# Two batches' agents in one key-score matmul, the agents' load put first, and a new order of the queues

## Chip, core and metric

The kernel runs on one core of a Trainium2 chip, as one launch. The metric is device time in microseconds of one execution; the kernel before takes 1118.79 us (median of 3 runs, 1118.47 to 1120.4).

## What is computed

Two stages, all in float32, for 2 batches of 12480 tokens with 128 channels and 49 agents per batch:

```python
scale = 1.0 / np.sqrt(128)
def sm(a, b):                               # softmax over b's rows
    s = scale * (a @ b.transpose(0, 2, 1)); s = s - s.max(-1, keepdims=True)
    e = np.exp(s); return e / (e.sum(-1, keepdims=True) + 1e-09)
agent_v = sm(agents, k) @ v                 # 49 x 128 per batch
x = (sm(q, agents) @ agent_v).reshape(24960, 128)
h = x @ w_in                                # 2048 wide
g = np.where(h >= 1, h, np.where(h <= -1, 0.0, (h + 1) ** 2 / 4))
out = g @ w_out
```

The kernel never forms x: it multiplies agent_v into w_in once per batch, and x @ w_in becomes (softmax of a query tile) times that product.

## The kernel before

**Stages.** For batch 0 the key phase (`keys_phase`) goes over the 98 subtiles of 128 keys in 14 groups of 7. A group's keys are loaded into one of four `kbuf` buffers (L453); `scores` (L473) multiplies each subtile, as the stationary operand, with the 49 agent columns `ag[:, b, :]` as the moving operand, into columns t*49 to t*49+49 of a PSUM tile. ScalarE copies the 343 columns out (`evac`, L284), VectorE takes their maximum (L485, L493). After the seventh group, and again after the last, the maximum over all keys is formed by a transpose (L515), a reduction, a diagonal matrix and a matmul (L528), so that GpSimd can subtract it (L567) and ScalarE take the exponential (L574). Then `av` (L582) multiplies the weights of each subtile (98 stationary columns) with 129 columns of `vbuf` (values and a column of ones; four buffers, L562), and VectorE adds the group's sum to `acc` (L598). `weights` normalizes (L621 to L623), transposes (L626), forms agent_v times w_in in four matmuls of 512 columns (L646) and splits the result into a high and a low part (L284, L658).

**Tiles.** Then 49 tiles of 512 tokens follow. `queries` loads a tile of q (L681), computes its scores against the agents (L686) and the softmax (L699 to L730), transposes it (L739). `pair` runs eight times per tile: `g1` (L782) makes 256 columns of h in a `ph` tile (three buffers of two PSUM banks); ScalarE does L789 and L794, VectorE L797; `g` is split into `ghi` (L284 on ScalarE, L288 on VectorE or L286 on GpSimd) and `glo` (L808, VectorE or GpSimd), and `g2h`, `g2l` (L818) accumulate three products in one of two PSUM banks. Batch 1's key phase runs in pieces between the pairs of batch 0's tiles, on the PSUM banks, with the same lines (`bank` in the profile in place of `ph`). Some preparation stands beside batch 0's key phase: `load_raw` (L405) fetches w_in and w_out as 64-bit words, and `decode` (L347 to L382) turns them into float32 on VectorE and GpSimd.

**Order.** Every step is an `Op` in `Order`; `run` puts the steps in one sequence by the time at which they could start in a planner's account, and among those by a key. `PRO`, `START` and `NEXT` hold the keys of the beginning and of batch 1, `KEYS0` and `KEYS1` those of the tiles of either batch, `HI_ENG` and `LO_ENG` the engine for each pair's split ("*" leaves it to the planner). Each engine then executes its instructions in that order. All loads and stores go through one queue, on SyncE (SP), which issues in order too and waits for a buffer where one is still in use. `warm` (L427) multiplies seven bf16 tiles of zeros at the very start.

A float32 matmul of the program stands as two records in the profile, each with a weight load of its own (98 matmuls of L473 per batch, 196 records).

Of the kernel before, what the change touches and what calls it, by code (L numbers as in the profile page):

```python
# [19 lines left out]
SUB = 128  # L20
# [3 lines left out]

HI_ENG = (("PA*P**DD", "DADAPPDA",), ("*DD*DDD*", "DPADDADD",))
LO_ENG = (("DDD*DD*P", "DDPDDDPD",), ("*PDD*PDD", "*DDD*D*D",))


ENG = dict(norm="PD", ql="P", qh="AD", mc="A", out="AD", sub="PD", evac="A")


KEYS0 = dict(g1=1.0, relu=9.2, square=-6.8, gate=11.9, hi=0.3, lo=-7.5, g2=8.3, g2l=6.0,
             out=19.0, q=-4.5, qm=-4.1, qe=28.0, qt=13.8, qn=34.9, qh=13.2, ql=-31.0, tr=13.9,
             mc=1.3)
KEYS1 = dict(g1=-1.4, relu=8.0, square=6.2, gate=8.7, hi=1.4, lo=-38.6, g2=11.0, g2l=-5.7,
             out=73.6, q=-4.4, qm=-27.9, qe=5.0, qt=2.6, qn=-4.0, qh=10.4, ql=3.9, tr=8.9,
             mc=28.3)
KEY = (KEYS0, KEYS1)  # L40


START = dict(raw0=-23.7, raw1=-33.2, raw2=-0.5, raw3=-25.1, out0=33.3, out1=100.6, out2=122.6,
             out3=110.6, q0=-50.6, q1=1.3, q2=145.1, v=9.6, dec=119.9, dout=240.7, km=32.2,
             qs0=85.1, qs1=101.4, qs2=186.4, sub=101.3, av=179.2, w=16.1, pm=108.3, split=7)


NEXT = dict(k=-30.3, v=171.3, s=0.7, step=2.8, m=81.8, av=92.2, avstep=6.7, sub=110.8, w=3.9)
WARM = 7
BUFS = dict(k=4, v=4, q=4, qs=3, m=2, g=5, hi=5, lo=5, o=2, wf=2, h=3)  # L50

# [35 lines left out]
class Order:  # L87
# [5 lines left out]
    def add(self, choices, fn, deps=(), key=0.0, acq=(), rel=()):  # L93

        if isinstance(choices[0], str):
            choices = (choices,)
        choices = tuple((e, us, bool(port)) for e, us, *port in choices)
        op = Op(len(self.ops), choices, fn, deps, key, acq, rel)
        self.ops.append(op)
        return op  # L100
# [82 lines left out]
def agent_attention_moe(  # L183
# [15 lines left out]
    nc = tc.nc  # L199
    C, NTOK = qT.shape  # L200
    B = kT.shape[0]
    A = agT.shape[2]
# [7 lines left out]
    A2 = 2 * A  # L210
# [21 lines left out]
    half = const.tile([128, 1], F32, name="half")  # L232
    idle = const.tile([128, 512], BF16, name="idle")
    ag = const.tile([128, B, A], F32, name="ag")
    win = const.tile([128, FF], F32, name="win")
    wo_hi = const.tile([128, NC, 128], F32R, name="wo_hi")
    wo_lo = const.tile([128, NC, 128], F32R, name="wo_lo")
# [27 lines left out]
    NSX = T // 128  # L265
    native = sorted({p for b in HI_ENG for e in b for p in range(NP) if e[p] == "N"})
    wo = {p: const.tile([128, 2, 128], F32, name=f"wo{p}") for p in native}
# [11 lines left out]
    add = od.add  # L279
# [20 lines left out]
    def one(ps):  # L300
        return ps if len(ps.shape) == 2 else ps[:, 0, :]
# [118 lines left out]
    PRO = -2000.0  # L420
# [9 lines left out]

    warm_op = add(("PE", 0.43 * WARM), warm, [first], PRO - 1, ("h",))
    warm_op.rel = (("h", warm_op),)
    ld_ag = add(("DMA", 0.2), lambda o, e: nc.sync.dma_start(out=ag, in_=agT), (), PRO - 0.5)


    def keys_phase(b, k_key, v_key, s_key, m_key, a_key, e_key, p_key=0.0, wait=None):

        on_bank = b > 0
        last, av_ops = None, []
        LK, LV, KX, KE = {}, {}, {}, {}  # L440
        first_of = [0] if b else [0, START["split"]]
        pms, mxs = [], []
# [4 lines left out]
        def part(g):  # L447
            return sum(g >= x for x in first_of) - 1
        for g in range(NG):
            kb = kbuf[(b * NG + g) % BUFS["k"]]  # L450

            def fn(o, e, g=g, kb=kb, h=slice(0, KG * SUB)):
                nc.sync.dma_start(out=kb[:, h], in_=kT[b, :, g * KG * SUB:][:, h])  # L453

            rest = []
            if b or g:
                LK[g] = load(128 * KG * SUB * 4, fn, (), k_key(g), ("k",))
            else:
                n, m = HALF * SUB, KG * SUB
                LK[g] = load(  # L460
                    128 * n * 4, lambda o, e, fn=fn: fn(o, e, h=slice(0, n)), (), k_key(g) - 1.0,
                    ("k",),
                )
                rest = [load(
                    128 * (m - n) * 4, lambda o, e, fn=fn: fn(o, e, h=slice(n, m)), (), k_key(g)
                )]

            def scores(o, e, g=g, kb=kb, lo=0, hi=HALF):
                if lo == 0:
                    area(o, ("k", b, g))  # L470
                ps = one(PS["k", b, g])
                for t in range(lo, hi):
                    nc.tensor.matmul(  # L473
                        out=ps[:, t * A:(t + 1) * A], lhsT=kb[:, t * SUB:(t + 1) * SUB],
                        rhs=ag[:, b, :], start=True, stop=True,
                    )

            def scores2(o, e, scores=scores):
                scores(o, e, lo=HALF, hi=KG)

            def evac(o, e, g=g):
                copy(e, ksf[:, g, 0:KG * A], one(PS.pop(("k", b, g)))[:, 0:KG * A])

            def gm(o, e, g=g):
                dve.tensor_reduce(  # L485
                    out=gmax[:, g % 2, :] if g else pms[0],
                    in_=ks[:, g, 0:KG, :].rearrange("p t a -> p a t"),
                    axis=AX.X,
                    op=ALU.max,
                )  # L490

            def gm2(o, e, g=g):
                dve.tensor_tensor(  # L493
                    out=pms[part(g)], in0=pms[part(g - 1)], in1=gmax[:, g % 2, :], op=ALU.max
                )

            x = add(("PE", 0.21 * HALF), scores, [LK[g], ld_ag], s_key(g))
            back = take(x, on_bank)
            y = add(("PE", 0.21 * (KG - HALF)), scores2, [x, *rest], s_key(g), (), (("k", LK[g]),))
            KE[g] = add(  # L500
                elementwise("evac", KG * A), evac, [y, *([wait[g]] if wait else [])], s_key(g) + 1, (), (back,)
            )
            KX[g] = add(("DVE", 0.42), gm, [KE[g]], s_key(g) + 1.1)
            if g:
                KX[g] = add(("DVE", 0.13, 1), gm2, [KX[g], KX[g - 1]], s_key(g) + 1.1)

        mb_ops, rescale = [], None
        for i in range(len(first_of)):

            pm, mx, mb = pms[i], mxs[i], mbs[i]  # L510
# [46 lines left out]
        for g in range(NG):  # L557
            vb = vbuf[(b * NG + g) % BUFS["v"]]
            s = ks[:, g, 0:KG, :]
# [40 lines left out]
            k = a_key(g)  # L600
# [70 lines left out]
    def queries(j):  # L671
        st, kk = {}, KEY[turn(j)]
        key = (j - 2) * NP + kk["q"] if j > 2 else PRO + START[f"qs{j}"]
        n, bl = width(j), blocks(j)
# [72 lines left out]

        lq = load(128 * n * 4, ld, (), key - 24 if j > 2 else PRO + START[f"q{j}"], ("q",))
        qs = add(("PE", 0.224 * ns), scores, [lq, ld_ag], key, ("qs",), (("q", lq),))
# [17 lines left out]
    def pair(j, p, w_ops, wo_op):  # L767
        s = j * NP + p
        st, kk = {}, KEY[turn(j)]
        hi_e, lo_e = plan(HI_ENG, j)[p], plan(LO_ENG, j)[p]  # L770
        n = width(j)
# [40 lines left out]
        def product(terms):  # L812
            for w, f, x, c in terms:
                first_mm = LEFT.get(j) is None
                if first_mm:
                    LEFT[j] = sum(2 if e == "N" else 6 for e in plan(HI_ENG, j))
                LEFT[j] -= 1
# [46 lines left out]
    def output(j):  # L864
# [19 lines left out]
        lambda g: PRO + g,  # L884
        lambda g: PRO + START["v"] + g,
        lambda g: PRO + 20 + g,
        PRO + START["km"],
        lambda g: PRO + START["av"] + 2 * g,
        lambda g: PRO + START["sub"] + 2 * g,
# [15 lines left out]
    for n in range(2):  # L905
        for h in range(2):
# [25 lines left out]
            k = PRO + START["dout"] + 2 * n + h  # L932
# [76 lines left out]
```

## Time and profile before

| | |
|---|---|
| median of 3 runs | 1118.79 us |
| the profiled execution | 1119.35 us, span 1117.6 us |
| PE busy | 1098.8 us, 98% of the span |
| ACT, DVE busy | 997.6 us, 993.6 us (89% each) |
| POOL busy | 589.1 us (53%) |
| moved by DMA | 56.57 MB, mean 51 GB/s |
| batch 0's key scores on PE | 10.15 to 57.17 us |
| batch 0's L582 on PE | 57.17 to 85.3 us |
| first L782 | 93.90 us |

The span runs from the first to the last instruction; the execution's own time is 1.75 us longer. PE's busy time counts modelled ends of pipelined matmuls, so the pace of a stretch is better read from the chain of waits, which gives the start, the length and the number of records of each piece.

### The profile page before, as it was taken

To read this page: it belongs to the slowest core of one execution; us is meant where nothing else is said; L and a number is where in the kernel's file an instruction comes from. 1 tells how busy PE (TensorE), PEld (TensorE's weight loads), DVE (VectorE), ACT (ScalarE), POOL (GpSimd) and SP (SyncE) were. 2 spreads that over 40 slices of the span, in tenths; PEclk is the share of its full clock that TensorE was granted. 3 is DMA by queue.
4 is the path that set the end of the run, shared out by engine and by line. 5 is a ranking of instruction groups with operands and counts; after the bars stand their busy time and mean duration, and the time that the engine had idled before them with its cause. 6 is when DMAs were issued, how large, how long until landed. Compare 5 with 4: busy or idle time off the path is not lost.

```text
span 1117.6 us, 15009 instructions
## 1 busy us (share of the span) xinstructions
PE 1098.8 (98%) x5357; PEld 911.0 (82%) x5357; DVE 993.6 (89%) x1203; ACT 997.6 (89%) x1165; POOL 589.1 (53%) x363
## 2 busy tenths in 40 slices
PE   7998999999999999999999999999999999999998
PEld 6986888888878887888878888888888888888776
DVE  5448898899998999988899989999999999999998
ACT  1226998999999999999989999999999999999997
POOL 2153554446577575455456464555555465565544
PEclk9998999999999999999999999999999999999999
DMA  7674221001001111211000000110010011000000
GB/s 237 232 259 146 69 69 38 28 19 38 20 29 52 55 50 39 63 36 45 29 20 29 29 29 19 30 38 20 19 39 20 23 34 36 10 10 20 10 20 17
DMA packets 23691, 56.57 MB, mean 51 GB/s; under 512 B 2752, under 2 KB 3136, under 8 KB 23616
## 3 DMA queue, kind: packets, MB, share of 16 engines
q1 hardware_dynamic: 23616, 55.60, 15.2%
q8 instruction: 43, 0.70, 0.3%
q14 instruction: 32, 0.26, 0.1%
HBM read 42.81 MB, written 12.78 MB: 50 GB/s over the span
## 4 chain that ended last, share of the span: by engine, by line
PE 90%; ACT 4%; DVE 3%; DMA 1%; issue 1%; SPq 0%; DVEq 0%; ACTq 0%
PE bank L818 45%; PE ph L782 31%; PE ph L473 4%; PE bank L686 3%; PE bank L473 2%; PE ph L582 2%; ACT g L789 2%; PE bank L582 2%; ACT g L794 1%; PE bank L739 1%; DVE g L797 1%; DVE glo L808 1%; ACT ghi L284 1%; DMA ag<-agT 1%; PE ph L646 1%
## 5 line engine op out<-in xcount | busy, mean ns | idle before, releaser
L808 POOL TENSOR_TENSOR glo<-g,ghi 128x1024 fp32r<-128x1024 f32 (+1 forms) x147 | 387.4, 2635 | 324.0 <-DVE ghi L288 281.3
L797 DVE SCALAR_TENSOR_TENSOR g<-g,ph 128x1024 f32<-128x1024 f32 (+1 forms) x392 | 467.0, 1207 | 55.6 <-ACT g L794 48.8
L789 ACT ACTIVATE g<-ph,half 128x1024 f32<-128x1024 f32 (+1 forms) x392 | 428.7, 1113 | 27.8 <-PE ph L782 25.5
L794 ACT ACTIVATE g<-g 128x1024 f32<-128x1024 f32 (+1 forms) x392 | 407.3, 1061 | 2.4
L782 PE MATMUL ph<-mt,w_hi 98*128 98x512 f32 (+3 forms) x800 | 317.9, 399 | 2.5 <-DVE g L797 2.3
L808 DVE TENSOR_TENSOR glo<-g,ghi 128x1024 fp32r<-128x1024 f32 (+1 forms) x245 | 312.3, 1300 | 3.0 <-ACT ghi L284 2.2
L782 PE MATMUL ph<-mt,w_lo 98*128 98x512 f32 (+3 forms) x800 | 312.4, 391 | 0.0
L818 PE MATMUL bank<-ghi,wo_hi 128*128 128x512 f32 (+1 forms) x784 | 249.5, 399 | 2.4 <-DVE acc L598 1.8
L818 PE MATMUL bank<-glo,wo_hi 128*128 128x512 f32 (+1 forms) x784 | 243.2, 395 | 0.9 <-POOL glo L808 0.9
L818 PE MATMUL bank<-ghi,wo_lo 128*128 128x512 f32 (+1 forms) x784 | 243.7, 392 | 0.0
L782 PEld LDWEIGHTS ph<-mt,w_hi 98*128 98x128 f32 x800 | 150.9, 189 | 40.1 <-DVE g L797 6.2
L782 PEld LDWEIGHTS ph<-mt,w_lo 98*128 98x128 f32 x800 | 151.6, 189 | 31.6 <-issue 0.2
L818 PEld LDWEIGHTS bank<-ghi,wo_lo 128*128 128x128 f32 x784 | 147.3, 188 | 33.1
L818 PEld LDWEIGHTS bank<-glo,wo_hi 128*128 128x128 f32 x784 | 145.2, 188 | 33.3 <-POOL glo L808 1.4
L818 PEld LDWEIGHTS bank<-ghi,wo_hi 128*128 128x128 f32 x784 | 142.6, 189 | 32.2 <-DVE acc L598 2.2
L288 DVE CAST ghi<-g 128x1024 fp32r<-128x1024 f32 (+1 forms) x199 | 139.5, 719 | 1.0
L284 ACT ACTIVATE ghi<-g 128x1024 fp32r<-128x1024 f32 (+1 forms) x122 | 128.6, 1055 | 4.6 <-DVE g L797 4.5
L286 POOL CAST ghi<-g 128x1024 fp32r<-128x1024 f32 x71 | 89.4, 1260 | 71.4 <-DVE g L797 47.0
L730 POOL TENSOR_TENSOR pq<-qd,pq 128x196 fp32r<-128x196 f32 (+1 forms) x49 | 37.3, 761 | 44.6 <-ACT pq L284 33.7
L686 PEld LDWEIGHTS bank<-ag,qt 128*128 128x128 f32 x368 | 47.9, 191 | 4.2 <-DVE acc L598 0.2
L473 PE MATMUL ph<-ag,kbuf 128*128 128x49 f32 x196 | 43.0, 413 | 5.8 <-DMA ag<-agT 5.8
L473 PEld LDWEIGHTS ph<-ag,kbuf 128*128 128x128 f32 x196 | 42.4, 332 | 6.8 <-DMA kbuf<-kT 6.7
(86 smaller groups left out, 609.4 us busy)
## 6 DMA issues: line engine op xcount, KB each, us to landing
vbuf<-v_in SPq DMA_DIRECT2D x28, 451.5 KB, 4.2
qt<-qT SPq DMA_DIRECT2D x48, 256.0 KB, 2.6
outT<-ot SPq DMA_DIRECT2D x48, 256.0 KB, 2.0
kbuf<-kT SPq DMA_DIRECT2D x27, 448.0 KB, 3.4
raw<-w_in SPq DMA_DIRECT2D x4, 512.0 KB, 6.6
raw<-w_out SPq DMA_DIRECT2D x4, 512.0 KB, 6.1
kbuf<-kT SPq DMA_DIRECT2D x1, 256.0 KB, 7.2
kbuf<-kT SPq DMA_DIRECT2D x1, 192.0 KB, 7.5
```

Source lines behind the costliest of these rows:

```text
L284: act.activation(out=out, in_=in_, func=ACTF.Copy)
L286: pool.tensor_copy(out, in_)
L288: dve.tensor_copy(out, in_)
L473: nc.tensor.matmul(out=ps[:, t * A:(t + 1) * A], lhsT=kb[:, t * SUB:(t + 1) * SUB], rhs=ag[:, b, :], start=True, stop=True,)
L582: nc.tensor.matmul(out=one(PS["v", b, g])[0:A2, 0:C + 1], lhsT=ksf[:, g, t * A:t * A + A2], rhs=vb[:, t, :], start=t == 0, stop=t == KG - 1,)
L686: nc.tensor.matmul(out=ps[lo:hi, i * A:(i + 1) * A], lhsT=st["q"][:, i * 128 + lo:i * 128 + hi], rhs=ag[:, b, :], start=True, stop=True,)
L782: nc.tensor.matmul(out=st["h"][:, c, lo:hi], lhsT=w[:, f:f + 128], rhs=M[j][:, lo:hi], start=(i == 0), stop=(i == 1),)
L789: act.activation(out=st["g"], in_=st["h"][:, :, 0:n], func=ACTF.Relu, bias=half, scale=0.5)
L794: act.activation(out=st["g"], in_=st["g"], func=ACTF.Square)
L797: dve.scalar_tensor_tensor(out=st["g"], in0=st["g"], scalar=1.0, in1=st["h"][:, :, 0:n], op0=ALU.min, op1=ALU.max,)
L808: (pool if e == "POOL" else dve).tensor_tensor(out=st["lo"], in0=st["g"], in1=st["hi"].bitcast(F32), op=ALU.subtract)
L818: nc.tensor.matmul(out=bank[j % 2][:, 0:n], lhsT=w[:, f, :], rhs=x[:, c, :], start=first_mm, stop=LEFT[j] == 0,)
```

## The change

`scores` moves 98 columns through each stationary key subtile in batch 0, both batches' agents side by side, and 49 as before in batch 1. Column block t*49 to t*49+98 is written; its second half is written again by the next subtile's matmul, and after the seventh it is not read. The load of the agents gets the first place of all (key 2*PRO in place of PRO - 0.5). The tables of the order and of the engines are filled with other numbers.

```diff
@@ tables
-HI_ENG = (("PA*P**DD", "DADAPPDA",), ("*DD*DDD*", "DPADDADD",))
+HI_ENG = (("P*P*PPD*", "PAD**DDA",), ("PDDPPDDA", "PP*DP*DA",))
...
@@ agent_attention_moe
     ag = const.tile([128, B, A], F32, name="ag")
+    agf = ag.rearrange("c b a -> c (b a)")
...
-    ld_ag = add(("DMA", 0.2), lambda o, e: nc.sync.dma_start(out=ag, in_=agT), (), PRO - 0.5)
+    ld_ag = add(("DMA", 0.2), lambda o, e: nc.sync.dma_start(out=ag, in_=agT), (), 2 * PRO)
...
                 ps = one(PS["k", b, g])
+
+
+                n = A if on_bank else A2
                 for t in range(lo, hi):
                     nc.tensor.matmul(
-                        out=ps[:, t * A:(t + 1) * A], lhsT=kb[:, t * SUB:(t + 1) * SUB],
-                        rhs=ag[:, b, :], start=True, stop=True,
+                        out=ps[:, t * A:t * A + n], lhsT=kb[:, t * SUB:(t + 1) * SUB],
+                        rhs=agf[:, b * A:b * A + n], start=True, stop=True,
                     )
```

Five lines come in ahead of most of the code, so that L473 of before is L478 now, L582 is L587, L686 is L691, L782 is L787 and L818 is L823. By engine the splits of `g` now stand thus: `ghi` 107 on ScalarE, 131 on VectorE, 154 on GpSimd (before 122, 199, 71), `glo` 282 on VectorE and 110 on GpSimd (before 245 and 147).

**PE, from the first matmul on real data into the key scores** (`kbuf_106` to `kbuf_109` are the four key buffers). Before:

```order
L473 MATMUL ph<-ag,kbuf_106 128x49 x4
L686 MATMUL ph<-ag,qt 128x49 x4
L473 MATMUL ph<-ag,kbuf_106 128x49 x3
L473 MATMUL ph<-ag,kbuf_107 128x49 x7
L686 MATMUL ph<-ag,qt 128x49 x4
L473 MATMUL ph<-ag,kbuf_108 128x49 x7
```

Now:

```order
L691 MATMUL ph<-ag,qt 128x49 x8
L478 MATMUL ph<-ag,kbuf_106 128x98 x7
L478 MATMUL ph<-ag,kbuf_107 128x98 x7
L478 MATMUL ph<-ag,kbuf_108 128x98 x7
L478 MATMUL ph<-ag,kbuf_109 128x98 x7
```

The scores of the first two query tiles stood between the first key groups and now stand ahead of them.

**SP, the queue's beginning** (`raw` are halves of w_in, `qt` query tiles, `ag` the agents). Before:

```order
L681 DMA qt_136<-qT 128x512
L405 DMA raw_158<-w_in 128x1024
L405 DMA raw_160<-w_in 128x1024
L405 DMA raw_158<-w_in 128x1024
L453 DMA kbuf0_106<-kT 128x512
L433 DMA ag_98<-agT 128x98
L405 DMA raw_160<-w_in 128x1024
L453 DMA kbuf0_106<-kT 128x384
L453 DMA kbuf1_107<-kT 128x896
L681 DMA qt_193<-qT 128x512
```

Now:

```order
L435 DMA ag_98<-agT 128x98
L407 DMA raw_149<-w_in 128x1024
L407 DMA raw_159<-w_in 128x1024
L686 DMA qt_161<-qT 128x512
L407 DMA raw_149<-w_in 128x1024
L686 DMA qt_172<-qT 128x512
L455 DMA kbuf0_106<-kT 128x512
L455 DMA kbuf0_106<-kT 128x384
L455 DMA kbuf1_107<-kT 128x896
```

The agents went from the sixth place to the first; the second query tile went ahead of the first keys, and the fourth piece of w_in behind the sixth key load.

**SP, the value loads of batch 0 after its last key load** (`vbuf0_110` to `vbuf3_113` are the four value buffers). Before:

```order
L562 DMA vbuf1_111<-v_in 128x903
L681 DMA qt_475<-qT 128x512
L562 DMA vbuf2_112<-v_in 128x903
L453 DMA kbuf2_108<-kT 128x896
L562 DMA vbuf3_113<-v_in 128x903
L562 DMA vbuf0_110<-v_in 128x903
L453 DMA kbuf3_109<-kT 128x896
L562 DMA vbuf1_111<-v_in 128x903
```

Now:

```order
L407 DMA raw_389<-w_out 128x1024
L567 DMA vbuf1_111<-v_in 128x903
L567 DMA vbuf2_112<-v_in 128x903
L567 DMA vbuf3_113<-v_in 128x903
L407 DMA raw_431<-w_out 128x1024
L407 DMA raw_389<-w_out 128x1024
L567 DMA vbuf0_110<-v_in 128x903
L567 DMA vbuf1_111<-v_in 128x903
```

Batch 1's first three key loads stood between the value loads of batch 0 and now stand behind the last of them; three of the four pieces of w_out stand among the value loads, all four of which stood ahead of the fifth.

## Rows read from the trace of the kernel before

**Rows 1.** The page: busy time by engine, and the chain that ended last.

```profile
PE 1098.8 (98%) x5357; PEld 911.0 (82%) x5357; DVE 993.6 (89%) x1203; ACT 997.6 (89%) x1165; POOL 589.1 (53%) x363
...
PE 90%; ACT 4%; DVE 3%; DMA 1%; issue 1%; SPq 0%; DVEq 0%; ACTq 0%
```

**Rows 2.** Windows: us, busy PE, PEld, DVE, ACT, POOL, clock, DMA share, GB/s.

```profile
10.00:57.00 47.00, 46.85 (x223) 46.69 (x223) 22.94 (x53) 8.83 (x20) 10.57 (x11) 1.00 0.66 223
...
104.00:108.00 4.00, 4.00 (x11) 3.13 (x10) 3.97 (x6) 4.00 (x6) 2.75 (x2) 0.50 0.37 115
...
112.00:116.00 4.00, 4.00 (x23) 3.43 (x22) 2.25 (x4) 2.85 (x5) 3.88 (x3) 1.00 0.37 109
```

**Rows 3.** Line L473: records, ns min/median/max, first and last start.

```profile
L473 PE MATMUL ph<-ag,kbuf x196: 388/413/451, 10.2 to 57.0; 128*128 128x49 f32 x196
...
L473 PE MATMUL bank<-ag,kbuf x196: 204/275/413, 85.1 to 198.7; 128*128 128x49 f32 x196
```

**Rows 4.** Chain in order of time, key stage: start us, us, what.

```profile
3.09 6.92 DMA ag<-agT
...
12.06 1.71 PE ph L686 x8
...
19.75 23.89 PE ph L473 x112
43.64 0.43 PE bank L739 x4
...
53.62 0.59 PE ph L528 x2
```

**Rows 5.** The same chain, at full-clock stretches and where it drops again.

```profile
107.10 1.71 PE ph L782 x4
...
109.39 1.50 PE bank L473 x14
...
113.72 0.94 PE ph L782 x4
114.66 0.83 PE bank L686 x8
...
118.35 0.26 PE bank L739 x4
```

**Rows 6.** Timeline of PE: start us, us, engine line op, count, [idle before].

```profile
1.19 3.17 PE L427 MATMUL ph<-idle 128*128 128x512 bf16 x7 [1.19 <-DVE idle L411]
...
57.17 4.13 PE L582 MATMUL ph<-vbuf,ks 128*98 128x129 f32 x18
...
60.90 2.17 PE L582 MATMUL ph<-vbuf,ks 128*98 128x129 f32 x17
...
100.26 0.47 PE L782 MATMUL ph<-mt,w_hi 98*128 98x512 f32 x1 [2.17 <-DVE g L797]
```

**Rows 7.** The same chain, batch 0's L582 stage at the full pace.

```profile
67.82 1.06 PE ph L686 x8
68.89 6.32 PE ph L582 x56
...
75.22 6.60 DMA vbuf<-v_in
```

**Rows 8.** DMA: a window of 4 us, and the key loads' time to landing.

```profile
8.00:12.00 4.00, 1.85 (x9) 1.88 (x10) 3.39 (x7) 0.00 (x0) 1.12 (x1) 1.00 1.04 402
...
kbuf<-kT SPq DMA_DIRECT2D x27, 448.0 KB, 3.4
```

**Rows 9.** The page's groups on GpSimd and VectorE; PE's waits after 101 us.

```profile
L808 POOL TENSOR_TENSOR glo<-g,ghi 128x1024 fp32r<-128x1024 f32 (+1 forms) x147 | 387.4, 2635 | 324.0 <-DVE ghi L288 281.3
...
L286 POOL CAST ghi<-g 128x1024 fp32r<-128x1024 f32 x71 | 89.4, 1260 | 71.4 <-DVE g L797 47.0
...
PE bank L818 <- DVE acc L598: 1.8, 1, 1.8
PE bank L818 <- POOL glo L808: 0.9, 1, 0.9
```

More of the change, by code (lines that the diff above doesn't have):

```diff
@@ L22 @@
 HALF = 4
-HI_ENG = (("PA*P**DD", "DADAPPDA",), ("*DD*DDD*", "DPADDADD",))
-LO_ENG = (("DDD*DD*P", "DDPDDDPD",), ("*PDD*PDD", "*DDD*D*D",))
+HI_ENG = (("P*P*PPD*", "PAD**DDA",), ("PDDPPDDA", "PP*DP*DA",))
+LO_ENG = (("PDDDDDPD", "DDPDD**D",), ("DPDDD*DD", "PDDDDDPD",))
 ENG = dict(norm="PD", ql="P", qh="AD", mc="A", out="AD", sub="PD", evac="A")
[L34 to L39, printed above, removed]
-KEY = (KEYS0, KEYS1)
[L43 to L48, printed above, removed]
+KEYS0 = dict(g1=0.8, relu=19.6, square=-12.2, gate=22.6, hi=-7.8, lo=-8.4, g2=7.3, g2l=7.6,
+             out=43.4, q=-4.1, qm=-28.3, qe=40.5, qt=20.8, qn=68.6, qh=-3.3, ql=-30.5,
+             tr=-27.7, mc=-2.1)
+KEYS1 = dict(g1=0.1, relu=28.3, square=-15.6, gate=22.5, hi=4.2, lo=-79.7, g2=6.5, g2l=-45.2,
+             out=129.1, q=-4.5, qm=-3.6, qe=9.5, qt=-29.8, qn=-10.8, qh=66.9, ql=-7.7, tr=11.8,
+             mc=11.7)
+KEY = (KEYS0, KEYS1)
+START = dict(raw0=-139.0, raw1=-44.8, raw2=-111.9, raw3=22.5, out0=62.6, out1=191.6,
+             out2=210.1, out3=149.5, q0=-25.7, q1=-103.9, q2=282.1, v=62.4, dec=84.9,
+             dout=246.4, km=-23.6, qs0=81.4, qs1=222.4, qs2=258.9, sub=142.0, av=192.9, w=25.3,
+             pm=171.0, split=7)
+NEXT = dict(k=-39.3, v=182.9, s=0.5, step=3.6, m=80.1, av=75.3, avstep=8.2, sub=147.4, w=-86.8)
 WARM = 7
```

## Prediction

> **What bounds the kernel now.** I read the page first: PE is busy for 98% of the span, and 90% of the chain that ended last is PE [rows 1]. So a microsecond counts where PE has idle time, or does its work slower than it could. Then the windows: in the 47 us of batch 0's key scores PE is busy almost without a gap, DVE for 22.94 us, ACT for 8.83 [rows 2]. Nothing holds PE up there; the question is its pace. The records of the line L473 answer it: with the same shape, 128x128 stationary and 49 columns moving, the median is 413 ns in this stage and 275 ns between 85 and 199 us [rows 3]. A record's length overlaps its neighbours, so I take the pace from the chain: 112 records in 23.89 us are 213 ns each [rows 4], later 14 in 1.50 us are 107 ns [rows 5]. The query scores L686, in both stretches too, show the same factor: 8 records take 1.71 us at 12 us and 0.83 us at 114 us [rows 4, 5].
>
> A factor of two is what the clock does. Between 104 and 108 us the granted clock reads 0.50, the lower level of 1.2 GHz, and four L782 take 1.71 us; at 1.00, which is 2.4 GHz, they take 0.94 [rows 2, 5]. In the key stage the granted clock reads 1.00 as well [rows 2], against all these durations. I take it that nothing was recorded before the first change of level, and that **the stage ran at 1.2 GHz**. When did it end? At 57.17 us L582 starts, with 129 moving columns: its first 18 records take 4.13 us, some 219 ns each, and of those that follow 17 take 2.17 us, 113 ns each or less [rows 6]. So the clock rose about 61 us, after 47 us of 49-column matmuls that did not raise it, seven bf16 matmuls at the start that did not either [rows 6], and 4 us of 129-column matmuls that did.
>
> **The change part by part.** The sum is against the profiled execution, 1119.35 us, which is 0.56 us above the median of the runs.
>
> *Columns.* Per matmul 98 columns move in place of 49, with the same weight load. What does a record cost then? At the lower level 49 columns take 213 ns and 129 columns 219 [rows 4, 6]; at the full one 107 [rows 5] and 113 (56 records of L582 in 6.32 us [rows 7]). Ninety-eight columns lie between these at both levels: at most 6 ns more per record, 196 x 6 = 1.2 us. The pace of 49 columns is hardly that of the columns, since 2.6 times as many add only 6 ns; so I take 0 and keep 1.2 us. What the change can bring is the clock, and no row shows 98 columns. I take it that the clock rises some 5 us into the key scores, about as long as L582 needed: 24 records at 213 ns, 172 at 107, a gain of 172 x 0.106 = 18.3 us. The eight transposes L739 go from 0.43 to 0.26 us per four, 0.3 us together [rows 4, 5]; the two small steps L515 and L528 give 0.3 (half of 0.59 for L528 [rows 4]). Together 18.9 us; the other end is nothing.
>
> *The beginning.* PE starts on real data when the agents land, sixth in the queue, at 3.09 + 6.92 = 10.0 us [rows 4]. Now they are first, but the first keys have the same three pieces of w_in ahead of them and a query tile more: 256 KB at 402 GB/s, 0.65 us [rows 8]. They land at about 10.7 us in place of about 10. The gain is elsewhere: the first query tile's scores run while these loads are under way, the second's from about 10.0 to 11.75, so that keys start at 11.8 and run through, without the two groups of 1.71 us in between [rows 4]. At the old pace the stage would end at 57.2 + 1.65 - 3.42 = 55.4 us: 1.8 us gained (1.1 if the second query tile lands 0.7 us later, 2.8 if the early loads come 1 us sooner).
>
> With the clock the key scores end at about 55.4 - 18.9 = 36.5 us. **What must keep up:** a key group then takes 14 x 0.107 = 1.5 us, and its 448 KB need 306 GB/s, below the 402 seen [rows 8]. A buffer is refilled 3.4 us after its issue [rows 8], and is wanted again three groups, 4.5 us, later; the fourth piece of w_in and one value load, some 1.2 us each at 402 GB/s, take most of that slack once each. DVE has 22.94 us of work in this stage [rows 2], which must now fit in about 25; PE waits for it only at the maximum after seven groups, which is asked for after the tenth. I cost both at nothing and keep 3 us upward.
>
> *The L582 stage.* From 57.2 to 85.3 us, 28.1 us. At the full pace 196 x 0.113 = 22.1, and 0.5 for the small steps L515 and L528, 22.6 us. The difference of 5.5 us is the 18 slow records (1.9 us [rows 6]), a query tile's scores of 1.06 us that now stand behind, and waiting for values: the chain runs through a value load of 6.60 us, issued at 75.22 us [rows 7], nearly twice the 3.4 us of a key load [rows 8]. The three key loads of batch 1 that stood among these loads are behind them now, with three pieces of w_out in their place, all of them in the first half. I take the whole 5.5 and keep 2.5 us of it as not won. The query tile's scores then cost 0.83 us later [rows 5].
>
> *After it.* The steps to the first pair are the same. Before the thirteenth L782 PE idled 2.17 us waiting for DVE [rows 6]; the new order puts 14 more key records of batch 1 ahead of that stretch's end, 1.5 us of work that has to be done anyway. I take 1.5 (0 to 2.2). From 101 us on PE's waits are single ones of 1.8 us and less [rows 9]; there is next to nothing to win, and I take 0, with 3 us either way.
>
> Sum: 18.9 + 1.8 + 5.5 - 0.8 + 1.5 = 26.9 us; 1119.35 - 26.9 = 1092.5, and 0.56 less by the median: **1092 us**. With the bounds (the clock some 16 records earlier or later is 1.7 us) this case reaches from 1087 to 1098.
>
> **The rivals.** *First: 98 columns do not raise the clock.* For it: 49 columns failed for 47 us, and after 103 us the clock stayed down beside 512-column matmuls, four L782 still taking 1.71 us at 107.10 [rows 5]. Against it: twice the columns move in the same time, nearer to L582's 129. Then 18.9 us fall away, and the slow start of L582 stays (1.9 us): 26.9 - 20.8 = 6.1 us gained, 1112.7 by the median. A clock that rises late, with the transposes L739 or near the stage's end, lies between this and the forecast.
>
> The Trainium skill speaks for this rival: "TensorE: Matmul & The Clock Gate", section "Why this matters for your kernels", has the full clock follow from keeping TensorE continuously busy. By that, columns would not matter in a stage that is busy throughout, and the sum would be this rival's 1112.7. The trace does not agree as it stands: PE was busy for 46.85 of 47.00 us and kept the lower pace [rows 2, 4].
>
> *Second, and slower: GpSimd holds up the pairs.* 154 `ghi` casts are GpSimd's in place of 71, at 1260 ns each [rows 9], 105 us more; 37 `glo` fewer at 2635 ns take 97 off. The load hardly changes, but a pair whose cast and `glo` both go to GpSimd has 3.9 us between `g` and its last product, and PE has waited 0.9 us for such a `glo` [rows 9]. With 30 waits like that in the 49 tiles the forecast's gain is gone (26.9 / 0.9), with 33 the kernel is slower by a measurable amount; one in every tile costs 44 us: 1136. Against it: it happened once after 101 us, in the old order, with more `glo` on GpSimd.
>
> *Third: the clock rises, but loads or DVE hold the key stage.* If each refill took 6.6 us as the late value load, four groups would take 6.6 + 1.5 = 8.1 in place of 6.0 us, 5 to 6 us over ten groups, 1098 us; it joins the forecast's upper end.
>
> **How the numbers follow.** Forecast, with the third case at its upper end, 0.62; first rival 0.28; second 0.10. The forecast's own range holds nine tenths of its 0.62; to reach 0.8 the range must take in most of the first rival, with 3 us above its time: 1086 to 1116. What a measurement can tell from no change is about 0.2%, 2.2 us. The forecast is faster, and the first rival in nearly nine of ten; the rest of it and a part of the second are no change: faster 0.86, same 0.05, slower 0.09.
>
> **What would show it.** Right: L478 with `ph` at about 107 ns a record from about 17 us on, a change to the higher level among the records of the granted clock there, L587 starting near 36 us and ending near 59, the first L787 near 67. Wrong, first rival: 196 records of L478 in some 42 us, L587 from 55 us, its first records at 219 ns. Second: PE's waits for `glo` from GpSimd in the tens, the early stages as forecast. Third: PE's waits for `kbuf` or for DVE between 17 and 40 us.

## The result, and the profile after

The changed kernel takes **1098.9 us** (median of 4 runs, 1098.55 to 1100.66) against 1119.5 for the kernel before beside it: the ratio is 0.9819, interval 0.9802 to 0.9836. That is 20.6 us less where 26.9 were forecast. The profiled execution took 1100.66 us, its span is 1097.8 us.

The page of the changed kernel, busy time and the chain that ended last, as in [rows 1]:

```profile
PE 1080.0 (98%) x5357; PEld 889.8 (81%) x5357; DVE 1020.8 (93%) x1176; ACT 991.5 (90%) x1146; POOL 614.1 (56%) x409
...
PE 82%; DVE 9%; issue 3%; ACT 3%; DMA 2%; POOL 0%; SPq 0%; POOLq 0%; DVEq 0%; ACTq 0%
```

PE is busy 19 us less with as many instructions: what it did, it did faster. VectorE is now at 93% and stands in the chain. Windows of the changed kernel, columns as in [rows 2]: batch 0's key scores, its L587 stage, and two stretches further on.

```profile
12.00:38.00 26.00, 24.55 (x203) 24.15 (x203) 20.34 (x47) 8.73 (x20) 8.96 (x10) 1.00 0.81 275
38.00:63.00 25.00, 24.13 (x207) 22.90 (x207) 15.18 (x37) 7.71 (x17) 14.65 (x16) 1.00 0.97 355
66.00:70.00 4.00, 3.87 (x5) 1.40 (x6) 3.31 (x8) 1.47 (x4) 1.38 (x1) 0.58 0.90 301
80.00:88.00 8.00, 8.00 (x24) 6.37 (x24) 6.89 (x7) 8.00 (x10) 4.58 (x3) 0.57 0.18 57
```

The key stage that took 47 us [rows 2] takes 26.7. The DMA engines, at 0.66 of their time there before, are busy for 0.81 of it, and for 0.97 of the L587 stage. After it the clock falls twice to its lower level, at 66.6 and 80.3 us (in the kernel before at 88.5 and 102.1). The chain of the changed kernel, beginning and first stages, against [rows 4, 7]:

```profile
2.11 6.06 DMA qt<-qT
8.17 0.14 issue
8.30 3.78 PE ph L691 x16
12.08 11.12 PE ph L478 x84
...
24.26 3.35 PE ph L478 x28
...
28.23 3.34 PE ph L478 x28
...
34.09 9.54 DMA raw<-w_out
...
43.73 0.43 DVE dhi L349
...
46.17 9.60 PE ph L587 x84
55.79 5.46 DMA vbuf<-v_in
```

PE's key scores are interrupted at 23 and 27 us, and in the L587 stage the chain leaves PE for a piece of w_out on which VectorE waits, and for a value load. The groups of L478 by form, against [rows 3]:

```profile
L478 PE MATMUL ph<-ag,kbuf x196: 274/275/497, 11.9 to 38.5; 128*128 128x98 f32 x196
...
L478 PE MATMUL bank<-ag,kbuf x196: 204/275/311, 63.8 to 204.3; 128*128 128x49 f32 x196
```

With 98 columns the median of a record is that of 49 columns at the full clock. The pace, taken from the start of one record to the start of the next, is 112 ns; the records themselves overlap.

| start of each, us of the span | before | forecast | after |
|---|---|---|---|
| batch 0's key scores | 10.15 | 11.8 | 11.88 |
| its L582 / L587 stage | 57.17 | 36.5 | 38.58 |
| end of that stage | 85.3 | 59.1 | 63.15 |
| first L782 / L787 | 93.90 | 68.5 by the sum | 71.81 |
| end of the span | 1117.6 | 1090.7 | 1097.8 |

### The profile page after: what moved, and what is told of

It reads as the page before. It is cut to its first block, busy times and chain, and to the rows that moved or that the text cites. A ratio compares the mean times of both kernels' runs of the same rounds, so it can differ in the third digit from the quotient of the medians.

```text
span 1097.8 us, 15155 instructions
## 1 busy us (share of the span) xinstructions
PE 1080.0 (98%) x5357; PEld 889.8 (81%) x5357; DVE 1020.8 (93%) x1176; ACT 991.5 (90%) x1146; POOL 614.1 (56%) x409
## 4 chain that ended last, share of the span: by engine, by line
PE 82%; DVE 9%; issue 3%; ACT 3%; DMA 2%; POOL 0%; SPq 0%; POOLq 0%; DVEq 0%; ACTq 0%
PE bank L823 42%; PE ph L787 29%; DVE g L802 4%; DVE glo L813 3%; PE bank L691 3%; PE bank L478 2%; PE ph L478 2%; PE bank L587 2%; ACT g L794 1%; PE ph L587 1%; PE bank L744 1%; ACT g L799 1%; DMA raw<-w_out 1%; PE ph L651 1%; DMA qt<-qT 1%
## 5 line engine op out<-in xcount | busy, mean ns | idle before, releaser
L813 POOL TENSOR_TENSOR glo<-g,ghi 128x1024 fp32r<-128x1024 f32 (+1 forms) x110 | 287.6, 2616 | 244.0 <-DVE ghi L290 211.3
L813 DVE TENSOR_TENSOR glo<-g,ghi 128x1024 fp32r<-128x1024 f32 (+1 forms) x282 | 379.7, 1373 | 2.8 <-ACT ghi L286 2.4
L787 PE MATMUL ph<-mt,w_hi 98*128 98x512 f32 (+3 forms) x800 | 318.1, 399 | 3.6 <-DVE g L802 3.5
L787 PE MATMUL ph<-mt,w_lo 98*128 98x512 f32 (+3 forms) x800 | 312.7, 392 | 0.0
L288 POOL CAST ghi<-g 128x1024 fp32r<-128x1024 f32 (+1 forms) x154 | 208.7, 1360 | 94.6 <-DVE g L802 70.5
L823 PE MATMUL bank<-ghi,wo_hi 128*128 128x512 f32 (+1 forms) x784 | 250.8, 401 | 0.0
L823 PE MATMUL bank<-glo,wo_hi 128*128 128x512 f32 (+1 forms) x784 | 245.7, 395 | 1.2 <-POOL glo L813 1.0
L823 PE MATMUL bank<-ghi,wo_lo 128*128 128x512 f32 (+1 forms) x784 | 243.3, 391 | 0.0
L787 PEld LDWEIGHTS ph<-mt,w_hi 98*128 98x128 f32 x800 | 150.9, 189 | 44.8 <-PE ph L787 6.3
L787 PEld LDWEIGHTS ph<-mt,w_lo 98*128 98x128 f32 x800 | 151.6, 190 | 31.3 <-issue 0.5
L823 PEld LDWEIGHTS bank<-ghi,wo_lo 128*128 128x128 f32 x784 | 147.5, 188 | 33.5
L823 PEld LDWEIGHTS bank<-glo,wo_hi 128*128 128x128 f32 x784 | 145.4, 188 | 32.4 <-POOL glo L813 1.3
L823 PEld LDWEIGHTS bank<-ghi,wo_hi 128*128 128x128 f32 x784 | 142.8, 189 | 29.1 <-issue 0.9
L286 ACT ACTIVATE ghi<-g 128x1024 fp32r<-128x1024 f32 (+1 forms) x107 | 113.0, 1056 | 11.9 <-DVE g L802 11.5
L290 DVE CAST ghi<-g 128x1024 fp32r<-128x1024 f32 (+1 forms) x131 | 92.5, 714 | 1.1 <-DVE g L802 0.5
L725 POOL TENSOR_TENSOR qd<-qd,qsm 128x196 f32<-128x196 f32 (+1 forms) x49 | 42.2, 862 | 42.3 <-DVE qsm L722 35.0
L691 PEld LDWEIGHTS bank<-ag,qt 128*128 128x128 f32 x368 | 48.0, 191 | 4.8 <-ACT w_hi L286 0.6
L691 PE MATMUL bank<-ag,qt 128*128 128x49 f32 x368 | 45.4, 266 | 0.0
```

The lines of the kernel that those rows point to most:

```text
L286: act.activation(out=out, in_=in_, func=ACTF.Copy)
L288: pool.tensor_copy(out, in_)
L290: dve.tensor_copy(out, in_)
L691: nc.tensor.matmul(out=ps[lo:hi, i * A:(i + 1) * A], lhsT=st["q"][:, i * 128 + lo:i * 128 + hi], rhs=ag[:, b, :], start=True, stop=True,)
L725: (pool if e == "POOL" else dve).tensor_tensor(out=d, in0=d, in1=st["sm"].unsqueeze(2).to_broadcast([128, ns, A]), op=ALU.mult,)
L787: nc.tensor.matmul(out=st["h"][:, c, lo:hi], lhsT=w[:, f:f + 128], rhs=M[j][:, lo:hi], start=(i == 0), stop=(i == 1),)
```

## The experiments

**The columns alone taken back, in the new order.**

```diff
-                n = A if on_bank else A2
+                n = A
```

> The changed kernel, but with 49 moving columns in batch 0's key scores as before; the order of all queues is that of the change. Theory (the columns raise the clock): the clock stays at the lower level through the key stage, 196 records of L478 at 213 ns in about 43 us from 11.9 us on, key stage ends near 55 us, the next stage starts at the slow pace; 1113 us. Rival (the new order and the agents' early load made the gain): the time stays within 2 us of the changed kernel's 1098.9.

Measured: 1117.43 us, ratio 0.9988 (0.9979 to 0.9997). Key scores from 12.15 to 55.75 us, the clock's rise at 61.1 us as before, first L787 at 90.51. Windows of this kernel, same columns:

```profile
12.00:56.00 44.00, 44.00 (x210) 43.81 (x210) 21.70 (x48) 9.39 (x23) 12.14 (x15) 1.00 0.64 210
57.00:84.00 27.00, 24.92 (x201) 24.16 (x200) 13.12 (x37) 5.84 (x13) 12.18 (x11) 1.00 0.79 263
```

PE is busy for every one of 44 us and keeps the slow pace, 213 ns a record; the 1.00 of the first window stands ahead of the first record of a change, at 61.1 us. So the columns are worth 18.5 us of the 20.6; the agents' load and the whole new order bring 1.6 us beside 49 columns. By the spans that is 3.4 us won up to the first L787 and 2.6 lost behind it (1026.3 us to the end in place of 1023.7).

**The columns alone, in the old order.** The same edit as in the diff of `scores`, nothing else.

> The kernel before with one edit, 98 moving columns in batch 0's key scores; tables and the agents' place in the queue as before. Theory (the columns raise the clock): the clock rises between 15 and 24 us, the key stage ends between 38 and 43 us in place of 57.2, and 14 to 18 us come off: 1101 to 1105 us. Rival (the order made the gain): 1117 us or more.

Measured: 1104.15 us, ratio 0.9862 (0.9841 to 0.9882): 14.9 us less than before, and the new order on top is worth 5.3. Windows of this kernel:

```profile
10.00:25.00 15.00, 15.00 (x71) 15.00 (x72) 9.56 (x23) 2.36 (x6) 3.17 (x4) 0.50 0.69 237
26.00:43.00 17.00, 16.08 (x142) 15.60 (x142) 12.84 (x29) 5.36 (x13) 4.87 (x7) 1.00 0.92 329
```

Here the lower level is recorded, from 8.0 to 25.1 us; in the changed kernel the clock rises at 15.4. In the old order two groups of query scores with 49 columns (1.84 us each) stand between the first key groups. The two effects are not independent: the order that is worth 1.6 us beside 49 columns is worth 5.3 beside 98.

**The agents' load alone put first, in the kernel before.**

```diff
-    ld_ag = add(("DMA", 0.2), lambda o, e: nc.sync.dma_start(out=ag, in_=agT), (), PRO - 0.5)
+    ld_ag = add(("DMA", 0.2), lambda o, e: nc.sync.dma_start(out=ag, in_=agT), (), 2 * PRO)
```

> The kernel before with one edit, the agents' load put first in the queue. Theory: the first keys stand behind the same loads as before and land at about 9.8 us, so PE starts 0 to 0.3 us earlier and the time is that of before, 1119 us. Rival (the agents held up the start, as the chain of waits has it): PE starts 2 us or more earlier and the time falls by as much, to 1117 us or less.

Measured: 1117.41 us, ratio 0.9985 (0.9976 to 0.9995), between the two. The key scores began no earlier (10.55 us, 10.15 before), but the first query tile's scores now ran ahead of them, at 4.15 us, and no longer between the key groups. The edit is one line, yet the planner also moved a few other pieces (eight L582 records stand ahead of the last key group). So the 1.7 us, about what the whole order brought beside 49 columns, belong to the load with what the planner made of it. One window of this kernel, over the key stage, answers to the first of [rows 2]:

```profile
10.00:57.00 47.00, 46.45 (x221) 46.27 (x222) 23.34 (x51) 9.62 (x22) 13.05 (x15) 0.50 0.67 227
```

The granted clock was 0.50 over the whole stage. In the kernel before the record began only at 61 us, and the page showed 1.00; its records have the same spacing, 213 ns, as those that ran at a recorded 0.50 here, so its key stage ran at the lower level.

**98 columns also in the first four key groups of batch 1**, on the changed kernel. The other batch's half is overwritten by the next subtile or left unread, as in batch 0.

```diff
+                if on_bank and g < WIDE:
+                    for t in reversed(range(KG - hi, KG - lo)):
+                        nc.tensor.matmul(
+                            out=ps[:, t * A:t * A + A2], lhsT=kb[:, t * SUB:(t + 1) * SUB],
+                            rhs=agf, start=True, stop=True,
+                        )
+                    return
...
-                copy(e, ksf[:, g, 0:KG * A], one(PS.pop(("k", b, g)))[:, 0:KG * A])
+                off = A if on_bank and g < WIDE else 0
+                copy(e, ksf[:, g, 0:KG * A], one(PS.pop(("k", b, g)))[:, off:off + KG * A])
```

> The changed kernel, and in addition 98 moving columns in the first four key groups of batch 1 (those that run before about 92 us); nothing is moved, the order on every engine is the same. Theory (the clock falls at 66.6 us and at 80.3 us because little moves through PE there, with 49-column scores among it): one or both falls are gone; each took some 1.7 and 3.4 us, so 1094 to 1097 us. Rival (PE's idle time makes the clock fall, whatever the columns): both falls stay and the time is that of the changed kernel, 1099 us.

Measured: 1096.04 us, ratio 0.9794 (0.9776 to 0.9813), 2.9 less than the changed kernel. Windows of this kernel, the two stretches in which the clock of the changed kernel falls:

```profile
66.00:70.00 4.00, 3.65 (x16) 1.86 (x14) 3.46 (x9) 2.02 (x5) 0.88 (x1) 1.00 1.01 384
80.00:88.00 8.00, 7.94 (x39) 6.38 (x38) 7.38 (x8) 8.00 (x10) 4.67 (x4) 1.00 0.20 57
```

No fall from the rise to the end, and in the 8 us of the second window PE starts 39 matmuls in place of 24. In the new order the falls behind the key phase came from the few columns moved there: this is the only edit, and the profiles of three later kernels that have it with the new tables of batch 0 show no fall either, while two without it do. (With all old tables it is otherwise, see below.)

**Two loads brought forward**, on the changed kernel: the fourth piece of w_in and the first value load go behind the load of key group 3, where the DMA engines stood idle.

```diff
+    early = [moved["raw"][3], moved["v"]]
+    ops = [o for o in ops if o not in early]
+    at = ops.index(moved["at"]) + 1
+    ops[at:at] = early
```

> The changed kernel with two loads moved in SP's order alone: the fourth piece of w_in and batch 0's first value load go right behind the load of key group 3, ahead of group 4's, into the stretch from 14 to 16 us in which the DMA engines stood idle; the order on PE, ACT, DVE and GpSimd is that of the changed kernel. Theory (between 22 and 36 us these two loads crowd the key loads, which makes the key scores wait 2.9 us over their pace of 112 ns a record): the key scores end 2 to 2.9 us earlier, near 36 us in place of 38.6, the first L787 comes 1.5 to 2.9 us earlier than 71.8, and the time is 1096 to 1097.5. Rival (it is the ScalarE copies of the key scores, which the list of waits names, that hold PE up): the key scores still end at 38.6 +- 0.3 and the time stays within 0.1% of the changed kernel's 1098.9.

Measured: 1098.86 us, ratio 0.9821 (0.9808 to 0.9834): no change. PE's waits of 10 to 64 us, first those of the changed kernel, then of this one (its L594 and L538 are L587 and L533):

```profile
PE ph L478 <- ACT mt L286: 0.8, 1, 0.8
PE ph L478 <- ACT ks L286: 0.6, 1, 0.6
PE ph L533 <- DVE factor L542: 0.3, 1, 0.3
PE ph L587 <- DMA vbuf<-v_in: 0.3, 1, 0.3
PE ph L587 <- DVE dhi L366: 0.2, 1, 0.2
```

```profile
PE ph L594 <- DVE acc L610: 0.7, 2, 0.4
PE ph L538 <- DVE factor L547: 0.3, 1, 0.3
```

The two waits of the key scores were put down to ScalarE, but the records of the loads show what they were: in the changed kernel the loads of the seventh and the ninth key group landed at 24.12 and 28.09 us, and PE went on at 24.26 and 28.23. In this run they are gone, though only in part by the edit. The clock rose at 18.9 us in place of 15.4, so PE came to the seventh group at 24.93, after its load, which landed no earlier than before (24.26); the ninth group's landed at 27.40. The key stage ends at 38.40 us, 0.2 earlier, and the L587 stage at 63.06, as without the edit. The theory named the wait rightly and its worth wrongly.

**The old tables of the tiles**, on the changed kernel (`HI_ENG`, `LO_ENG`, `KEYS0`, `KEYS1` as in the kernel before).

> The changed kernel with the four tables of the query tiles (HI_ENG, LO_ENG, KEYS0, KEYS1) of the kernel before; the agents' load, the 98 columns and the order of the beginning and of batch 1's key phase stay as changed. Theory (the new tables of the tiles lose 2 to 3 us in the steady stage, through waits of PE for VectorE): from the first L787 to the end 1023.6 us as in the kernel before, in place of 1026.0, the key stage as in the changed kernel, and 1095 to 1097. Rival (what is lost after the first pair belongs to batch 1's key phase or to the clock's two falls, not to the tables): the stretch stays at 1025.5 to 1026.5 and the time at 1098.9 +- 1; or the old tables, made for another start, cost more: above 1100.

Measured: 1124.09 us, ratio 1.0049 (1.0034 to 1.0064): slower than the kernel before. From the first L787 to the end it takes 1046.9 us, against 1026.0 with the new tables and 1023.7 in the kernel before with these same ones. The theory that the new tables lose falls in this form; the rival's last case held: under the new beginning the old tables cost 25 us. A planner makes the sequence from the tables and from what came ahead, and the same tables gave another sequence here: of the `ghi`, 127 fell to ScalarE, 191 to VectorE and 74 to GpSimd (122, 199 and 71 in the kernel before).

**Wide groups and early loads together**, and **both with the old tables**.

> Two edits of other runs together, on the changed kernel: 98 moving columns also in the first four key groups of batch 1, and the fourth piece of w_in with batch 0's first value load behind the load of key group 3. If the first is worth 2.9 us (measured) and the second 2 to 2.9 us and they act in different stretches, they add up: 1093 to 1094.5. If the early loads bring nothing: 1096 +- 0.7, as with the first edit alone. The clock shows no fall after its rise.

> The same two edits with the tile tables of the kernel before as well. If the new tables lose 2 to 3 us in the steady stage whatever the clock does: 1090.5 to 1092.5. If what the tables seem to lose came from the two falls of the clock, which the wide key groups of batch 1 remove already: the same as without the old tables, within 1 us. From the first L787 to the end 1021 us by the first and 1023.3 by the second.

Measured: 1095.32 us, ratio 0.9788 (0.9775 to 0.98), and 1122.06 us, ratio 1.0023 (1.001 to 1.0036). The first is the fastest kernel of the study; that the early loads help it is not shown (1096.04 without them, and the intervals overlap). The second repeats the miss of the old tables, and its profile shows a fall of the clock at 78.7 us in spite of the wide groups.

**The old tables for batch 1's tiles alone**, on the fastest kernel.

> The kernel with wide key groups in batch 1 and early loads (1095.3 us), with the tables of batch 1's tiles alone (HI_ENG, LO_ENG, KEYS of batch 1) as in the kernel before. From the 401st record of the line g1 to the end's 800th, batch 1's tiles take 481.1 us in the kernel before and 484.8 in the changed one. Theory (batch 1's new tables, which give VectorE 23 us more to do, lose these 3.7 us): 1091 to 1092.5. Rival (a table serves only the sequence of work it was chosen with, as the run with all old tables suggests, where this stretch took 498 us): 1100 to 1110.

Measured: 1108.26 us, ratio 0.99 (0.9886 to 0.9913). The rival held: batch 1's tiles took 495.7 us with these tables, 484.8 with the new ones.

**Twelve casts of batch 1 from VectorE to ScalarE**, on the fastest kernel, at the same places of the sequence.

```diff
+    for o in [o for j, o in moved["hi"] if j > 24 and o.engine == "DVE"][::6]:
+        o.engine = "ACT"
```

> The kernel with wide key groups in batch 1 and early loads (1095.3 us), with every sixth of the ghi casts that VectorE does in batch 1's tiles (12 of 73) done by ScalarE, at the same place of the sequence; nothing else moves. Theory (VectorE, 98.8% busy there, is what PE's pace in batch 1's tiles hangs on): 12 casts of 0.68 us off VectorE shorten the tiles of batch 1 by 1 to 4 us, 1091.5 to 1094.3. Rival (VectorE is full but not what ends last, or ScalarE with 12.7 us more takes its place): 1095.3 +- 0.7 or slower.

Measured: 1101.61 us, ratio 0.9844 (0.983 to 0.9857), 6.3 us slower; batch 1's tiles took 491.2 us. VectorE's busy time between 700 and 800 us went from 98.81 to 94.67 us, and PE did not gain by it. PE's waits of this kernel from 600 us on:

```profile
PE bank L760 <- ACT ot L287: 3.8, 9, 0.4
PE ph L803 <- DVE g L818: 3.5, 13, 0.8
```

The second is what it was without the edit (3.3 us in 12 waits); the first is new: ScalarE's copy of the output tile now comes late. Less load on VectorE alone did not help. Whether a full VectorE set the pace is not settled by it, since ScalarE had 12.7 us more to do, as the rival had it.

**98 columns in both batches, in the old order**: the kernel before with the edits of the second and the fourth experiment.

> The kernel before with 98 moving columns in batch 0 (1104.2 us) and also in the first four key groups of batch 1. If the two falls of the clock behind batch 0's key phase come from the few columns moved there, they go here too, and 2.9 us with them: 1101.2, clock at the higher level from its rise to the end; the new order is then worth 5 us, with the wide groups in both. If in the old order something else stands in those stretches: falls as before, 1104.

Measured: 1098.64 us, ratio 0.9824 (0.9803 to 0.9845). The profiled execution alone took 1103.22 us, with a fall of the clock from 83.5 to 90.3 us; the other three took 1097.54 to 1098.69. Of the two falls of the old order one is gone and one stays although 98 columns move in these groups, so there the few columns are not the whole of it. Beside wide groups in both batches the new order is worth 2.6 us (1096.04; the intervals just overlap), not 5. From 608 us on PE has no wait above 1 us here.

**No decode of w_out on VectorE**, on the changed kernel.

```diff
+        if skip:
+            first = exponent = top = least = power = rest = lambda o, e: None
```

> The changed kernel without the 24 VectorE instructions that turn the four pieces of w_out into float32 (w_out is left out of the computation; GpSimd's and ScalarE's steps of it stay, on other data, and all loads and the order of the rest are the same). In the changed kernel the L587 stage takes 24.6 us in place of 22.6, its group 4 starts 1.06 us late behind a VectorE that waits in order for a w_out piece, and a step of 1.21 us stands between the last sum and the normalization. Theory (w_out's decode in VectorE's order among the sums holds PE): the L587 stage takes 22.3 to 23.2 us, the first L787 comes 2 to 3.5 us earlier after the stage's start, 1095.5 to 1097. Rival (value loads beside w_out's loads hold it): 24.6 +- 0.5 us, 1098.9 +- 0.8.

Measured: 1098.42 us, ratio 0.9818 (0.9805 to 0.9832): no change. The L587 stage (L593 here) took 24.8 us. PE's waits of this kernel from 36 to 75 us, and a window of its stage:

```profile
PE ph L593 <- DMA vbuf<-v_in: 1.5, 3, 0.6
PE ph L484 <- DMA kbuf<-kT: 0.8, 1, 0.8
PE ph L657 <- DVE avT L640: 0.4, 1, 0.4
```

```profile
39.00:63.00 24.00, 22.53 (x196) 21.58 (x195) 6.48 (x21) 6.96 (x15) 14.75 (x16) 1.00 0.91 314
```

VectorE's work in the stage fell from 15.18 us (of 25) to 6.48 (of 24), and the stage did not get shorter. The rival held.

## Why the prediction was right, and which terms were not

**The clock, right.** The forecast took the slow key stage for the lower level of the clock, against a page that read 1.00, and the runs recorded 0.50 there. It assumed that 98 columns raise it: they did, 3.5 us into the key scores where 5 were assumed. (The other eight profiles of the new order with 98 columns have 4.7 to 6.9 us, so the 3.5 is in part luck.) Their worth was forecast as 18.9 us and 1.9 for the slow start of the L582 stage, 20.8 together, and measured as 18.5; the first rival falls. The pace of a record is 112 ns, not 107, 0.9 us over the stage; but 49 columns of batch 1 have a spacing of 112 ns as well (the 107 took in a short first step), so the extra columns cost nothing, as assumed. The rule of the Trainium skill that spoke for the rival ("TensorE: Matmul & The Clock Gate", section "Why this matters for your kernels": the full clock follows from keeping TensorE continuously busy) is not borne out here. PE was busy for 44.00 of 44.00 us with 49 columns and stayed slow; with 98 the clock rose, in a stage in which PE was busy for 24.55 of 26.00. The columns were the only edit between the two. One reading of the forecast does not hold in every execution: that the seven bf16 matmuls at the start did not raise the clock. In five of the fourteen profiles they did, until PE had stood idle (see the last section). No term hung on it.

**The beginning, right in size.** The key scores began at 11.88 us (11.8 forecast), and with 49 columns ended at 55.75 (55.4 forecast). The agents' load put first gave 1.7 us in the old order. What the forecast did not see: with the query scores out of the way the clock also rises earlier, at 15.4 to 18.9 us in the nine kernels with 98 columns in the new order and at 25.1 and 25.5 in the two in the old one. That this is why the order is worth more beside 98 columns is likely; no run took it apart.

**The cover of the key stage, failed, 2.1 us.** "I cost both at nothing and keep 3 us upward", of loads and VectorE. The seventh and the ninth key group began 0.14 us after their loads had landed, and lost 1.8 us by it, beyond the four transposes that stand ahead of the seventh. So the third rival held in kind, at 1.8 us in place of 5 to 6. The slack was worked out from a landing time of 3.4 us, that of the kernel before, with DMA engines at 0.66 in this stage; at 0.81 these two loads took 5.62 and 6.46. Key scores ended at 38.58 in place of 36.5: 1.8 of waits and 0.9 of pace, less 0.8 for the earlier rise, leave 0.2 open.

**The L582 stage, mis-sized by 2.0 us.** 24.6 us in place of 22.6. The change of order was to win all the waits of this stage. At the old pace of the key scores it won next to nothing: 27.9 us with 49 columns, 28.1 before, where the forecast's slow-clock case had some 24.5. And at the new pace the loads of two shortened stages follow closely on each other. In the kernel before, the DMA engines were busy for 0.80 of the stage that [rows 7] show a part of:

```profile
57.00:85.00 28.00, 26.17 (x208) 25.19 (x208) 13.10 (x37) 8.15 (x19) 14.42 (x17) 1.00 0.80 276
```

Now it is 0.97. The records of the loads show the hold: in the changed kernel the fifth, 11th, 12th and 14th of the 14 groups start at 46.16, 55.96, 57.76 and 61.39 us, and their value loads landed 0.13 to 0.14 us before, at 46.02, 55.83, 57.63 and 61.25 (for the first of them the chain names VectorE). Against the pace these four lose some 1.7 us. A value buffer is loaded again when its group is done, and is wanted again three groups, 4.7 us, later; these refills took 4.0 to 5.7 us. Loads brought forward did not end the stage sooner (five groups start so behind a landing there), nor did a VectorE without the decode (four); with 49 columns it is two. So value loads released the late groups. What would land them sooner, fewer bytes beside them or another order, was not tried.

**After it, wrong in sign.** The term was +1.5 and 0 for the steady stage; from the first pair to the end the changed kernel takes 1026.0 us in place of 1023.7, 2.3 more. It is batch 1's tiles: from the 401st of 800 L787 with `w_hi` to the last, 484.8 us against 481.1, while batch 0's gained 1.1. With 49 columns in the new order they take 485.0, with 98 in the old one 481.1: the loss belongs to the new order with its tables, not to the columns. PE's waits of the changed kernel from 85 us on, against the last of [rows 9]:

```profile
PE ph L787 <- DVE g L802: 3.5, 13, 0.8
PE bank L823 <- POOL glo L813: 1.0, 1, 1.0
```

Twelve of the thirteen short waits for `g` are new (the kernel before has one of 0.2 us), and together they come near the loss. VectorE's `glo`, 600 to 1085 us, before and after (busy us, mean ns, idle before):

```profile
L808 DVE TENSOR_TENSOR glo<-g,ghi 128x1024 fp32r<-128x1024 f32 x111 | 136.5, 1254 | 0.5 <-ACT ghi L284 0.4
```

```profile
L813 DVE TENSOR_TENSOR glo<-g,ghi 128x1024 fp32r<-128x1024 f32 x147 | 200.0, 1399 | 0.0
```

There are more of them and each is longer. The forecast looked only at GpSimd's own lateness, for its second rival; that one got a single wait of 1.0 us and falls. What it left out is what GpSimd's casts do to VectorE: a `glo` that finds a GpSimd instruction running takes the rest of that one and 1.08 us more, in place of 1.21 (see the last section). Worked out from the records, this lengthens VectorE's `glo` between 600 and 1085 us by some 28 us, where it was 4 in the kernel before. Twelve of the thirteen waits stand behind a `glo` so lengthened, with VectorE never idle in between. One such wait in the timelines of GpSimd (the cast), VectorE (the late `glo`, and the `g` behind it) and PE:

```profile
658.84 1.87 POOL L288 CAST ghi<-g 128x1024 fp32r<-128x1024 f32 x1 [0.57 <-DVE g L802]
```

```profile
659.74 2.06 DVE L813 TENSOR_TENSOR glo<-g,ghi 128x1024 fp32r<-128x1024 f32 x1
661.72 0.35 DVE L704 TENSOR_REDUCE qmx<-bank 128x4 f32<-128x196 f32 x1
661.99 1.20 DVE L802 SCALAR_TENSOR_TENSOR g<-g,ph 128x1024 f32<-128x1024 f32 x1
663.12 0.35 DVE L707 TENSOR_TENSOR qd<-bank,qmx 128x196 f32<-128x196 f32 x1
663.39 2.33 DVE L802 SCALAR_TENSOR_TENSOR g<-g,ph 128x1024 f32<-128x1024 f32 x2
```

```profile
664.74 0.47 PE L787 MATMUL ph<-mt,w_hi 98*128 98x512 f32 x1 [0.23 <-DVE g L802]
```

So the likely cause of the 3.7 us is the casts that the new tables give GpSimd, 87 in batch 1's tiles in place of 13. It is read from the traces and not shown by a run: none took these casts off GpSimd in the order as it stands, and the run that took 12 casts off VectorE left the waits.

**The account.** By spans: 26.9 forecast, less 2.1 at the end of the key scores, 2.0 in the L587 stage and 3.8 after the first pair (−2.3 in place of +1.5), and plus the 0.8 that the displaced query scores were priced at and that did not show (from the stage's end to the first pair 8.7 us, 8.6 before), is 19.8; the spans differ by 1117.6 − 1097.8 = 19.8. The mechanism was right. The sum was too high because both stages' waits were taken at nothing and the tiles' order at its best: 1098.9 us lies just above the 1087 to 1098 that the forecast's own case allowed, and inside the stated range, which was widened towards the first rival.

## What to carry to other kernels

Where a matmul that moves few columns runs at twice its time, first find out which level of the clock it ran at, by the spacing of equal records, since the page can read full speed there; columns added to a matmul whose pace is not that of its columns cost nothing here and brought the clock up, also after the key phase (another 2.9 us). When a stage becomes nearly twice as fast, price its loads at the share that the DMA engines will then have, not at the landing time of the slow stage, and against the time until the buffer is wanted again. When the profile names an engine for a wait, look at when the load landed as well. When work goes to GpSimd, look at what VectorE does beside it, not only at when GpSimd is done. A table that orders a planner's work belongs to the sequence it was made with: keep or replace all of it, and measure an order term beside the other edit, since here it was worth 1.6 us without it and 5.3 with it.

## What was not expected of the hardware

- The clock's rise in the key stage came at 15.4 to 18.9 us in the profiled runs of nine kernels (the changed one and eight of the experiments) whose matmuls are the same up to there. At 213 against 112 ns a record, these 3.4 us are some 1.6 us of time.
- The record of the clock begins at its first change. In five profiles of fourteen (the kernel before with 98 columns, with the agents first and with both batches wide; the twelve casts; no decode) that is a rise at 4.5 to 5.0 us, behind the seven bf16 matmuls, and a fall at 7.9 to 8.4 us with PE idle; these alone show the lower level ahead of the later rise. With the agents first, eight records of query scores stand across the early rise (first line, PE's timeline) and are faster than the eight that came at 17 us (second line). Their spacing goes from 213 to 110 ns. Below, two windows of the same kernel on either side of the fall.

```profile
4.15 1.44 PE L686 MATMUL ph<-ag,qt 128*128 128x49 f32 x8
...
16.97 1.91 PE L686 MATMUL ph<-ag,qt 128*128 128x49 f32 x8
```

```profile
5.00:8.00 3.00, 0.59 (x5) 0.46 (x4) 1.44 (x5) 0.10 (x1) 0.00 (x0) 1.00 0.90 263
9.00:12.00 3.00, 1.45 (x7) 1.45 (x8) 3.00 (x7) 0.37 (x1) 1.32 (x3) 0.50 1.05 417
```

- VectorE's `glo` has a median of 1.22 us and a longest of 3.43. Worked out from the records of both engines between 610 and 1090 us in the changed kernel, for the 141 of 128x1024: 49 that began while a GpSimd instruction had 0.16 to 2.36 us left took that rest and 1.07 to 1.08 us, every one of them; 24 that began ahead of a GpSimd instruction took 1.19 to 1.22, and the others 1.21 to 1.22. Its `g`, which reads PSUM, had a median of 1.21 in either case. That GpSimd holds VectorE up there is a reading of these records; no run took GpSimd away. The Trainium skill, "SBUF — State Buffer", section "SBUF: two separate sides", describes such a thing: a VectorE instruction with two inputs in SBUF and a GpSimd instruction that reads SBUF exclude each other for their whole length. The records agree with it, the rest and 1.08 us for `glo`, whose two inputs are in SBUF.
